# A layernorm–MLP kernel: tile 0's transposes copied in quarters by two engines, tile 2's statistics on ScalarE in place of tile 1's, another product order in the last group, and another packing seed

## Chip, cores, metric

One core of one Trainium2 chip. The metric is the device time of one execution in microseconds, lower is better. A "span" is what the profile of one execution covers; it is about 1.7 us less than the time of that execution. In the lines of a profile PE is TensorE (PEld its weight loads), DVE is VectorE, ACT is ScalarE, POOL is GpSimd; SBUF is the memory for tiles, PSUM the one that TensorE's products are written to.

## The reference

```python
def _layernorm(x, axis=-1, eps=1e-5):
    m = jnp.mean(x, axis=axis, keepdims=True)
    v = jnp.var(x, axis=axis, keepdims=True)
    return (x - m) / jnp.sqrt(v + eps)

def reference(x, w1, b1, w2, b2):        # x (1, 2048, 1024) bf16, w1 (1024, 3584), w2 (3584, 1024)
    y = _layernorm(x, axis=-1)
    h = gelu_tanh(jnp.einsum("bsd,df->bsf", y, w1) + b1)
    return jnp.einsum("bsf,fd->bsd", h, w2) + b2
```

## The kernel before

Both matrix products are done with one level of a seven-product scheme (seven block products P1 to P7 in place of eight, with sums of blocks by VectorE), so VectorE is nearly as busy as TensorE. x comes in 16 tiles of 128 rows. A tile is normalized on VectorE (statistics in two halves, aggregate, plus epsilon; the power -1/2 on GpSimd; then one `tensor_scalar`), or its two moments are taken by ScalarE. The first four tiles are then transposed by TensorE and copied out of PSUM; this is the head.

The program is a list of tasks. A list scheduler fixes each engine's order at build time, from durations and due times written into the kernel, and a packing step with a seed chooses where the buffers lie in SBUF. A buffer that lies on an earlier one's place has to wait for that one's readers.

```python
ACT_LN = (1, 8, 10, 12, 14)       # tiles whose moments ScalarE takes
SEED = 11                          # of the packing
...
def to_yT_pe(b, i, bank, other=None):            # transposes of tile i by TensorE
    ...                                          # tile 0: two halves in banks 7 and 6; others: one bank
    for h in range(2):
        op("ACT", A_CP, lambda e, h=h: e.copy(out=yy[:, h * KH:(h + 1) * KH, t * P:(t + 1) * P],
                                             in_=pv[h][:, h * KH:(h + 1) * KH, :]), ...)
...
elif q == 7:                                     # Wino.step: one product, and what hangs on it
    self.prod(7, Y, False)
    s3 = save(Y, n + "s3", mem=MA)               # ScalarE, PSUM to SBUF
    add(Z, Z, s3, n + "V")                       # VectorE
    if self.last:
        self.s3 = s3
    else:
        MA.free(s3)
    self.sink["22"](Z)                           # output sum and store
elif q == 4 and self.last:                       # last group: P4 as two half tiles
    self.sink["21"](Y, (self.prod, self.s3, (X, (X + 4) % 8)))
...
pr.due = (None, 5.0)                             # the head
norm(0)
pr.due = None
for i in range(1, 4):
    norm(i)
for bank in range(7):
    warm(1, bank=bank, full=True)                # matmuls on ones, to warm TensorE up
warm(20)
for n, c in ((8, c_st[0][0]), (8, c_mv[0]), (6, c_rstd[0])):
    warm(n, c)
to_yT_pe(0, 0, 7, 6)
warm(5, bank=5)
...
flat += [(last, 7), (last, 3), (last, 4)]        # end of the order of products
```

## Time and profile before

| | before |
|---|---|
| time, median of 3 | 335.25 us (335.22 to 335.66) |
| span of the profiled execution | 333.3 us |
| T0, T1, T2 (first weight load of the transposes of tiles 0, 1, 2; the row of their matmuls starts up to 0.06 later) | 6.84, 8.59, 11.32 us |
| M, the first 512-column matmul (the head is over) | 16.49 us |
| E, the end of the last matmul (modelled) | 330.17 us |
| middle, E - M | 313.68 us |
| tail, span - E | 3.1 us |

I cut the time at M and E because the three parts have different causes.

### The profile page before, as it was taken

How to read it: one execution, taken by the hardware profiler on the slowest of the kernel's cores; microseconds unless marked ns; L12 is line 12 of the kernel's file. 1: busy time of each engine (PE TensorE's matmuls, PEld its weight loads, DVE VectorE, ACT ScalarE, POOL GpSimd, SP SyncE). 2: the span in 40 equal slices, each digit the busy share in tenths (PEclk: the TensorE clock that was granted, in tenths of full speed). 3: DMA queues.
4: the chain of work that ended last, by engine and by line, in shares of the span. 5: the costliest groups of instructions: out<-in, count | busy, mean ns of one | idle time of the engine just before them, and what ended most of it. 6: DMA issues, size and time to landing. Idle time of an engine off the chain costs nothing.

```text
span 333.3 us, 6014 instructions
## 1 busy us (share of the span) xinstructions
PE 328.5 (99%) x2328; PEld 220.0 (66%) x2328; DVE 295.9 (89%) x480; ACT 180.9 (54%) x307; POOL 13.0 (4%) x29
## 2 busy tenths in 40 slices
PE   8999999999999999999999999999999999999996
PEld 5844444444444444444446888888888888888885
DVE  5879999999999959968979994999999999999735
ACT  5597999997676776777765555543021222222010
POOL 2210121100000000000000000000000000000000
PEclk9999999999999999999999999999999999999999
DMA  7997999989989998999958462654846547659642
GB/s 228 326 221 183 281 270 328 326 205 305 314 268 365 325 339 260 352 350 325 301 158 245 130 202 76 190 147 141 238 154 187 162 129 208 202 157 269 177 118 63
DMA packets 103622, 76.88 MB, mean 231 GB/s; under 512 B 16426, under 2 KB 94890, under 8 KB 103594
## 3 DMA queue, kind: packets, MB, share of 16 engines
q1 hardware_dynamic: 103034, 76.18, 78.1%
q8 instruction: 18, 0.29, 0.4%
q10 hardware_dynamic: 560, 0.33, 0.3%
q14 instruction: 10, 0.08, 0.1%
HBM read 48.96 MB, written 24.38 MB: 220 GB/s over the span
## 4 chain that ended last, share of the span: by engine, by line
PE 95%; DMA 2%; DVE 1%; SPq 1%; issue 0%; ACT 0%; DVEq 0%
PE ps L891 49%; PE ps L1158 44%; DMA mem<-in_x_dram 2%; PE ps L1220 1%; SPq L754 0%; DVE mem L1078 0%; DVE st_sb L661 0%; PE ps L694 0%; SPq L637 0%; DVE mem L1121 0%; ACT mem L820 0%; DVE mem L670 0%; SPq L634 0%; DVEq L562 0%; PE ps L1180 0%
## 5 line engine op out<-in xcount | busy, mean ns | idle before, releaser
L891 PE MATMUL ps<-mem 128*128 128x512 f16 x756 | 164.3, 379 | 0.0
L1158 PE MATMUL ps<-mem 128*128 128x256 f16 (+1 forms) x1372 | 150.4, 273 | 0.0
L1158 PEld LDWEIGHTS ps<-mem 128*128 128x128 f16 x1372 | 134.2, 98 | 16.4
L891 PEld LDWEIGHTS ps<-mem 128*128 128x128 f16 (+1 forms) x756 | 73.4, 98 | 89.2 <-ACT mem L820 1.4
L820 ACT COPY mem<-ps 128x512 f32<-128x512 f32 x111 | 64.8, 588 | 80.1 <-PE ps L1158 65.5
L804 ACT ACTIVATE mem<-ps,b_sb 128x512 f16<-128x512 f32 x112 | 74.1, 692 | 23.4 <-DVE ps L828 14.2
L828 DVE TENSOR_TENSOR ps<-ps,mem 128x512 f32<-128x512 f32 x84 | 58.3, 693 | 19.3 <-ACT mem L820 19.1
L1048 DVE TENSOR_TENSOR mem<-mem 128x1792 f16<-128x1792 f16 x56 | 59.7, 1083 | 0.9 <-PE ps L1158 0.4
L957 DVE TENSOR_TENSOR mem<-mem 128x512 f16<-128x512 f16 (+5 forms) x84 | 37.0, 461 | 2.7 <-DMA w_scr<-mem 1.4
L765 DVE TENSOR_TENSOR mem<-mem 128x1024 f16<-128x1024 bf16 (+1 forms) x56 | 37.6, 684 | 1.7 <-DMA mem<-in_w_dram 1.6
L1059 DVE TENSOR_TENSOR mem<-mem 128x1792 f16<-128x1792 f16 x32 | 33.9, 1083 | 0.1
L811 ACT COPY ps<-ps 128x512 f32<-128x512 f32 x31 | 17.7, 570 | 27.2 <-PE ps L1158 25.2
L661 DVE BATCH_NORM_STATS2 st_sb<-mem 128x6 f32<-128x512 bf16 x22 | 14.4, 681 | 4.8 <-DMA mem<-in_x_dram 4.8
L1078 DVE TENSOR_TENSOR mem<-ps,mem 128x512 bf16<-128x512 f32 (+1 forms) x25 | 16.2, 663 | 2.7 <-PE ps L1158 2.6
L941 DVE TENSOR_TENSOR mem<-mem 128x2048 f16<-128x2048 bf16 (+1 forms) x16 | 17.3, 1084 | 0.1
L1091 DVE TENSOR_TENSOR mem<-ps,mem 128x512 f32<-128x512 f32 x24 | 16.2, 683 | 0.2
L731 DVE TENSOR_TENSOR mem<-mem 128x512 f16<-128x512 f16 x32 | 12.1, 420 | 1.9 <-DMA mem<-mem 1.7
L667 POOL TENSOR_TENSOR rstd_sb<-vpe_sb,nhalf 128x1 f32<-128x1 f32 x11 | 7.8, 713 | 43.4 <-DVE vpe_sb L664 43.4
L1180 PE MATMUL ps<-ones 128*128 128x128 bf16 (+1 forms) x55 | 6.8, 290 | 1.1 <-POOL ones L603 1.1
L1220 PE MATMUL ps<-mem 128*128 128x128 f16 x112 | 7.3, 219 | 0.2 <-ACT mem L704 0.2
L1220 PEld LDWEIGHTS ps<-mem 128*128 128x128 bf16 x112 | 6.4, 98 | 0.6 <-ACT mem L704 0.5
L856 ACT COPY ps<-mem 128x512 f32<-128x512 f32 x11 | 6.5, 590 | 0.3
(31 smaller groups left out, 59.8 us busy)
## 6 DMA issues: line engine op xcount, KB each, us to landing
mem<-in_w_dram SPq DMA_DIRECT2D x80, 256.0 KB, 4.9
mem<-w_scr SPq DMA_DIRECT2D x28, 448.0 KB, 3.5
w_scr<-mem SPq DMA_DIRECT2D x21, 512.0 KB, 5.0
w_raw<-mem SPq DMA_DIRECT2D x12, 512.0 KB, 5.4
mem<-w_raw SPq DMA_DIRECT2D x12, 448.0 KB, 4.5
mem<-in_w_dram SPq DMA_DIRECT2D x9, 448.0 KB, 4.5
mem<-in_x_dram SPq DMA_DIRECT2D x15, 256.0 KB, 4.4
out_dram<-mem SPq DMA_DIRECT2D x30, 128.0 KB, 2.6
```

The costliest lines, as they stand in the source:

```text
L765: op("DVE", d_tt(n), lambda e: e.tensor_tensor(out=o[0], in0=a[0], in1=bb[0], op=f), r=[a[1], bb[1]], w=[o[1]], name=f"w1S{k}_{ch}")
L804: op("ACT", A_GELU, lambda e: e.activation(out=dst, in_=bank2(bank), func=ACT.Gelu_apprx_tanh, bias=b1_sb[:, f:f + 1], scale=1.0), r=[bank ...
L811: op("ACT", A_CP, lambda e: e.copy(out=banks[dst][:, :], in_=banks[src][:, :]), r=[bank_c[src]], w=[bank_c[dst]], name=name, lat=A_LAT)
L820: op("ACT", A_CP, lambda e: e.copy(out=v16(a, 0, 2048, F32), in_=banks[src][:, :]), r=[bank_c[src]], w=[a.c()], name=name, lat=A_LAT)
L828: op("DVE", D_PS, lambda e: e.tensor_tensor(out=banks[dst][:, :], in0=banks[src][:, :], in1=v16(a, 0, 2048, F32), op=ALU.add), r=[bank_c[s ...
L891: i = e.matmul(banks[bank][:, :], lhsT=lv[:, k, :], rhs=rv[:, k, :], start=(fresh and k == 0), stop=(k == KH - 1), skip_group_check=True)
L941: op("DVE", d_tt(2 * self.n), lambda e: e.tensor_tensor(out=vd, in0=va, in1=vb, op=ALU.subtract), r=self.cells(a) + self.cells(bb), w=self ...
L957: tt = lambda o, a, c: (lambda e: e.tensor_tensor(out=o, in0=a, in1=c, op=ALU.subtract))
L1048: op("DVE", d_tt(UN // 2), lambda e: e.tensor_tensor(out=v16(t), in0=a[0], in1=bb[0], op=f), r=a[1] + bb[1], w=[t.c()], name=f"in{b}_{p}{q}")
L1059: op("DVE", d_tt(UN // 2), lambda e, va=va, vb=vb, vd=vd: e.tensor_tensor(out=vd, in0=va, in1=vb, op=f), r=h_cells(b, a, u, s) + h_cells(b ...
L1158: i = e.matmul(bank2(bank)[:, t, :], lhsT=av3[:, k, t * P:(t + 1) * P], rhs=bv[:, k, :], start=(fresh and t == ts[0] and k == 0), stop=(t ...
L1220: i = e.matmul(banks[r][:, t * P:(t + 1) * P], lhsT=lv[:, k, :], rhs=rhs[:, k, t * P:(t + 1) * P], start=(t == 0 and k == 0), stop=(k == K ...
```

## The change

Its intent, as far as the code tells it: tile 2's normalization no longer stands behind tile 3's load (ScalarE takes tile 2's moments, and the loads go 0, 2, 1, 3); the first transposed tile reaches its matmuls sooner through four quarter copies, two on ScalarE and two on VectorE; and after the last product little is left to do, because P6 and P7, which other sums hang on, come early in the last group and P3, P4 come last.

```diff
-ACT_LN = (1, 8, 10, 12, 14)
+ACT_LN = (2, 8, 10, 12, 14)
-SEED = 11
+SEED = 1
+HEAD_LN = (5.0, 7.3, 9.3, 13.5)
+TE_DUE = 7.1
 ... (eps of a tile on ScalarE: VectorE in place of GpSimd for i < 8)
-            def to_yT_pe(b, i, bank, other=None):
+            def to_yT_pe(b, i, where):
 ...
+                        if j % 2:
+                            op("DVE", 0.11 + m * P / 960, lambda e, src=src, dst=dst: e.tensor_copy(out=dst, in_=src), ...)
+                        else:
+                            op("ACT", 0.15 + m * P / 1400, lambda e, src=src, dst=dst: e.copy(out=dst, in_=src), ...)
 ...
-            pr.due = (None, 5.0)
-            norm(0)
+            for i in range(4):
+                pr.due = (None, HEAD_LN[i])
+                norm(i)
             pr.due = None
-            for i in range(1, 4):
-                norm(i)
 ...
-            to_yT_pe(0, 0, 7, 6)
+            pr.due = (None, TE_DUE)
+            to_yT_pe(0, 0, (7, 6, 5, 4))
 ... (V waits for P5 and P7, whichever is later; s3 kept accordingly)
             flat += [(last, 7), (last, 3), (last, 4)]
+            prev = c_seq[-2]
+            flat[-10:] = [(last, 1), (prev, 7), (last, 6), (prev, 4), (last, 7), (prev, 3), (last, 5), (last, 2), (last, 3), (last, 4)]
 ...
-                    put(i - (IN_LA if q != 3 else 4), lambda b=b, p=p, q=q: in_sum(b, p, q))
+                    at_ = min(i, flat.index((g, 6)) - 1) if q == 5 else i
+                    put(at_ - (IN_LA if q != 3 else 4), lambda b=b, p=p, q=q: in_sum(b, p, q))
```

## The prediction

> **What bounds the kernel now.** I read the page's busy shares first, then the chain that ended last in order of time, then the timeline of the first 17 us, then that of the last 10 us. The busy shares say that the tensor engine is nearly always at work; the chain says where that is not so.
>
> ```profile
> PE 328.5 (99%) x2328; PEld 220.0 (66%) x2328; DVE 295.9 (89%) x480; ACT 180.9 (54%) x307; POOL 13.0 (4%) x29
> ```
> ```profile
> 3.77 5.68 DMA mem<-in_x_dram
> 9.45 0.02 issue
> 9.47 1.28 DVE st_sb L661 x2
> 10.76 0.45 DVE mem L670
> ...
> 16.65 12.95 PE ps L891 x60
> ...
> 63.51 114.29 PE ps L891 x528
> ...
> 186.51 140.62 PE ps L1158 x1288
> 327.13 0.02 issue
> 327.15 0.59 ACT mem L820
> ```
>
> The columns are start, length, engine and line. From 16.65 to 327.13 the chain never leaves PE: 528 matmuls of 512 columns in 114.29 us are 216 ns each, 1288 of 256 columns in 140.62 us are 109 ns each, with no gap. The change alters neither their number nor their shape, so nothing is to be won in those 310 us; it can only be lost. What can move is the head (16.65 us) and what follows the last matmul. In the head the chain runs through the load of x tile 3 (landed at 9.45) and its two statistics on DVE, because the normalization of tile 2 stands behind them in DVE's order: DVE sat 0.94 us waiting for that load, and PE was ready for tile 2's transposes about 0.4 us before it got them.
>
> The timeline of the head (start, length, engine, line, operation; DVE, POOL and PE rows picked):
>
> ```profile
> 5.48 0.15 DVE L664 TENSOR_SCALAR vpe_sb<-mv_sb 128x1 f32<-128x1 f32 x1
> 5.55 0.69 DVE L661 BATCH_NORM_STATS2 st_sb<-mem 128x6 f32<-128x512 bf16 x1
> 5.71 0.56 POOL L667 TENSOR_TENSOR rstd_sb<-vpe_sb,nhalf 128x1 f32<-128x1 f32 x1 [4.17 <-DVE vpe_sb L664]
> 6.31 0.74 DVE L670 TENSOR_SCALAR mem<-mem,mv_sb,rstd_sb 128x512 f16<-128x512 bf16 x2
> 6.84 0.49 PEld L694 LDWEIGHTS ps<-ident,mem 128*128 128x128 f16 x8
> ...
> 7.96 0.67 PEld L1220 LDWEIGHTS ps<-mem 128*128 128x128 bf16 x12 [0.35 <-ACT mem L704]
> 8.00 0.54 DVE L656 TENSOR_SCALAR mem<-mem,mv_sb,rstd_sb 128x1024 f16<-128x1024 bf16 x1
> 8.59 0.49 PEld L694 LDWEIGHTS ps<-ident,mem 128*128 128x128 f16 x8
> ...
> 11.32 0.46 PEld L694 LDWEIGHTS ps<-ident,mem 128*128 128x128 f16 x8 [0.51 <-issue]
> ```
>
> The reader is to see three starts on PE: T0 (tile 0's transposes) 6.84, T1 8.59, T2 11.32. After T2 PE hardly waits, so **the start of T2 is the head's measure**. The timeline of the tail:
>
> ```profile
> 327.77 0.70 DVE L828 TENSOR_TENSOR ps<-ps,mem 128x512 f32<-128x512 f32 x1 [1.45 <-ACT mem L820]
> 328.38 0.68 DVE L1121 TENSOR_TENSOR mem<-mem 128x512 f32<-128x512 f32 x1
> 328.98 1.94 DVE L1078 TENSOR_TENSOR mem<-ps,mem 128x512 bf16<-128x512 f32 x4
> ```
>
> Product P7 ends at 327.13 and what hangs on it (save by ACT, add V, add of s3, four output sums) keeps DVE busy without a gap up to 330.92. PE's last row starts at 304.79 and lasts 25.38, so PE ends at 330.17. The last half-tile sum takes 0.41 us (rows by form), so it started at 330.51: 0.34 us after PE, because of the queue on DVE.
>
> **What the Trainium skill says.** "SBUF — State Buffer", section "Who interferes with whom": DVE and GpSimd share one pair of ports as an exclusive lock. The trace agrees where it shows it: the pow on POOL beside tile 1's normalization took 0.78 us (8.16), the others 0.55 to 0.56. "VectorE: DVE Perf Modes", section "Why PSUM operands drop a tier": a PSUM operand excludes the two-port mode. So the new DVE copies out of PSUM should not hold up POOL; no row of before shows a 16-bit PSUM copy on DVE. "Perfetto Trace Analysis", section "Tensor Engine Instruction (MATMUL, LD_WEIGHTS)": the end of a matmul in a profile is an estimate. Here an output sum began at 325.63, 0.03 us after the end that the chain implies for its product (327.13 less one product of 14 matmuls by 109 ns = 1.53), so the estimate serves within some hundredths.
>
> **The change, part by part.** I took the new order of each engine from the build of the changed kernel (an order, not a time).
>
> *Head, first tile.* DVE did: statistics 0, aggregate 0, eps 0, one half statistic of tile 2, norm 0 (two halves), other half, and so on. It will do: statistics 0, aggregate, eps, both half statistics of tile 1, norm 0. ACT takes tile 2 in place of tile 1 at the same place; tile 2 is now loaded second, tile 1 third, tile 3 fourth, ahead of all weights. Statistics start 0.60 us apart (9.47 to 10.68 for two), so from 5.55 the two are through at 6.76; norm 0 could start at 6.31 and now starts at 6.76. **T0 slips by 0.45, to 7.29.** It gains in copying: first group of matmuls came 1.12 us after T0 (6.84 to 7.96), through a copy of 512 columns. Now ACT copies quarter 0 and DVE quarter 1. A 512-column ACT copy takes 0.59, a 28-column one 0.24, so 256 columns take about 0.41 (interpolated). DVE: norm halves at 6.76 and 7.09, aggregate 7.42, eps 7.67, so the copy starts about 7.75; at 0.41 (the 256-column sum out of PSUM) it ends 8.16. First wave matmul about 8.23, against 7.96: later by 0.27, the quarters giving back 0.18 of 0.45.
>
> *Tile 1.* eps start to norm start is 0.83 on this path (5.48 to 6.31), so with eps 1 at 7.67, norm 1 can start at 8.50; the two DVE copies end about then. Norm 1 to T1 was 0.59 (8.00 to 8.59): T1 at 9.09, 0.50 later than before. After T1: 0.45 to the next matmuls, but the matmuls of tile 1 need its ACT copy, 1.33 after T1 (8.59 to 9.92): 10.42. Then 12 + 4 matmuls at 0.056 (28 in 1.56) make 0.89, so PE is ready for T2 at 11.31.
>
> *Tile 2.* Its statistics are done on ACT at about 6.85. eps 2 follows norm 1 (about 9.05), norm 2 about 9.9, ready at 10.5: no longer late. So T2 starts when PE gets there, 11.31, against 11.32. **Head: gain 0.0.** The wait behind tile 3 goes, and what took its place is the wait for tiles 0 and 1.
>
> *Weights.* Tile 3 now goes ahead of the first weights. Summing bytes moved in half-microsecond windows, the seventh 0.26 MB piece (tile 3 before) passes at 8.1 us and landed at 9.45, 1.3 later; the second passes at 3.85 and landed at 4.42. The first weight tile moves from fourth to fifth place: passes at 6.5, lands about 7.5; the second passes 7.3, lands about 8.5, used at about 8.7. Tight, but I count no wait.
>
> *Tail.* PE's work is the same, its order is P3, then both halves of P4 last, with P5 and P2 ahead of them and P6, P7 long done. Counting back from PE's end E in products of 1.53: P5 ends E-4.59, P2 E-3.06, P3 E-1.53. DVE: W and V from E-4.56 to about E-3.3, the P2 sum from E-3.03, the Z sum E-2.4 to E-1.7, the P3 sum E-1.5 to E-0.8, first half of P4 E-0.74 to E-0.33, then idle until the last half at E+0.03. The start moves from E+0.34 to E+0.03. **Tail: gain 0.31.** The first half of P4 reuses the bank that the P2 sum reads; that is free at about E-2.4, before E-1.53, so no wait.
>
> *Sum:* 0.0 - 0.31 + 0.0 for the middle: 335.25 - 0.31 = 334.94, said as 334.95.
>
> **The rivals.** *A: the slip of norm 0 is absorbed and the head gains.* If tile 1 or 2's data or the POOL steps come sooner, T2 can come up to about 0.4 us earlier, as the wait of 0.36 to 0.51 in front of it goes: 334.5 or so. For it: the change was evidently aimed at that wait. Against: the static order puts both statistics ahead of norm 0, and rows above show no slack of 0.45. *B: weights become the wait.* Fifth to eighth place is later by about 0.8 us each; if the second or third weight tile lands at 9 rather than 8.5, the wave stalls 0.2 to 0.5: about 335.3. The bytes above speak for a near miss. *C: the buffers are packed with another seed, and loads and DVE sums in the middle stand in another order.* DVE is busy 48.91 of 50 us from 50 to 100, so a late load could reach PE. Against it: ACT and PE wait nowhere long in before, and the units for the last group still have some 5 us in hand by the order. It would cost 0.2 to 1 us: 335.2 to 336.
>
> **Range and chances.** The head is uncertain by about 0.3 either way, the tail by 0.1, runs differ by 0.1 to 0.4 (335.22 to 335.66), and C adds a little on the slow side. I take 334.5 to 335.4. Two per cent are 6.7 us; the head's idle and the tail together hold less than that, so faster by 2% is almost excluded (0.01), slower by 2% would need a hang-up in the middle (0.01), within 2% is 0.98.
>
> **What would show it.** T0 near 7.3, first wave near 8.2, T1 near 9.1, T2 near 11.3, no DVE wait for tile 3; the chain no longer through tile 3's load but through tile 0's and 1's statistics; at the end the last two half sums apart, the last starting within 0.1 us of PE's end; PE without gaps between. The prediction is wrong if T2 moves by more than 0.3 us, if a wave waits for weights, or if the middle shows a PE gap.

## More of the kernel before

The middle can be read off one view, the timeline of TensorE alone (start, length, engine, line, operation, count, and in brackets idle time with what ended it):

```profile
16.49 13.11 PE L891 MATMUL ps<-mem 128*128 128x512 f16 x60
29.44 0.38 PE L1180 MATMUL ps<-ones 128*128 128x512 bf16 x1
29.65 148.16 PE L891 MATMUL ps<-mem 128*128 128x512 f16 x684
```

A row ends where TensorE waits or the line changes. One row of 684 matmuls without a bracket means that the profile shows no wait of TensorE there.

## The result

| | before | after |
|---|---|---|
| time, median of 6 runs each | 335.37 us (335.00 to 335.66) | 335.02 us (334.73 to 335.33) |
| ratio | | 0.999, 95% interval 0.9977 to 1.0003 |
| span of the profiled execution | 333.3 us | 333.3 us |
| T0, T1, T2 | 6.84, 8.59, 11.32 | 7.80, 9.65, 11.80 |
| M | 16.49 | 16.99 |
| E - M | 313.68 | 313.73 |
| span - E | 3.1 | 2.6 |

A ratio here is the mean time of one kernel's fast runs over the mean of the other's in the same rounds, so it is not quite the ratio of the medians quoted beside it. The predicted 334.95 and its range hold. In the profiled execution, however, the head lost 0.50 us, which was not predicted, and the tail gave 0.55 back (0.19 of it by chance, as shown below), so the two spans are equal. The experiments had to say which of the two is the change and which is luck.

TensorE's row of 684 is unbroken in this profile too, with the same length:

```profile
30.15 148.19 PE L903 MATMUL ps<-mem 128*128 128x512 f16 x684
```

The chain that ended last, after:

```profile
1.74 4.38 DMA mem<-in_x_dram
6.12 0.02 issue
6.15 1.29 DVE st_sb L664 x2
7.43 0.64 DVE mem L673 x2
...
9.67 0.60 PE ps L700 x8
...
17.15 12.95 PE ps L903 x60
...
187.05 143.68 PE ps L1170 x1316
330.73 0.02 issue
330.75 0.42 DVE mem L1090
```

It no longer passes through tile 3's load. It begins with the third x load (now tile 1), its two statistics and norm 0 (7.43), as the prediction expected of the new order; but the load landed at 6.12, and the prediction had put the start of these statistics at 5.55. At the end one half-tile sum of 0.42 stands behind the last matmul. Before, the chain left TensorE already at P7 (327.13, some 3 us ahead of the last matmul), and a save, two adds and four sums that hang on P7 reached past it.

The timeline of the head, after (VectorE, ScalarE, GpSimd and TensorE rows picked):

```profile
6.15 1.29 DVE L664 BATCH_NORM_STATS2 st_sb<-mem 128x6 f32<-128x512 bf16 x2 [0.83 <-DMA mem<-in_x_dram]
...
7.80 0.72 PE L700 MATMUL ps<-ident,mem 128*128 128x128 f16 x8 [0.80 <-DVE mem L673]
...
8.13 0.70 ACT L712 COPY mem<-ps 128x256 f16<-128x256 f16 x2 [1.43 <-PE ps L700]
...
8.29 0.56 DVE L709 COPY mem<-ps 128x256 f16<-128x256 f16 x2
...
8.46 0.55 POOL L670 TENSOR_TENSOR rstd_sb<-vpe_sb,nhalf 128x1 f32<-128x1 f32 x1 [2.50 <-DVE vpe_sb L667]
...
8.64 0.84 PE L1233 MATMUL ps<-mem 128*128 128x128 f16 x12
```

VectorE sat idle 0.83 us for the load, and TensorE then 0.80 us for norm 0. The quarters work: the copies lie side by side, and the first group of matmuls (8.64) comes 0.84 after T0, against 1.12 before.

The timeline of the tail, after:

```profile
327.70 1.29 DVE L1090 TENSOR_TENSOR mem<-ps,mem 128x512 bf16<-128x512 f32 x2
329.23 1.19 DVE L1090 TENSOR_TENSOR mem<-ps,mem 128x512 bf16<-128x512 f32 x2 [0.24 <-PE ps L1170]
330.75 0.42 DVE L1090 TENSOR_TENSOR mem<-ps,mem 128x256 bf16<-128x256 f32 x1 [0.34 <-PE ps L1170]
```

VectorE idles 0.34 us before the last half sum: it waits for TensorE, and no longer TensorE's result for it. TensorE's last row ends at 330.72, so the sum starts 0.03 after it and ends 0.45 after it. Before, the last half sum ended 0.74 after TensorE's end.

### The profile page after: what moved, and what is told of

It is laid out like the page before. It is cut to its first block, busy times and chain, and to the rows that moved or that the text cites. A ratio compares the mean times of both kernels' runs of the same rounds, so it can differ in the third digit from the quotient of the medians.

```text
span 333.3 us, 6020 instructions
## 1 busy us (share of the span) xinstructions
PE 328.6 (99%) x2328; PEld 220.0 (66%) x2328; DVE 296.6 (89%) x483; ACT 180.3 (54%) x307; POOL 13.8 (4%) x28
## 4 chain that ended last, share of the span: by engine, by line
PE 96%; DMA 1%; DVE 1%; SPq 0%; POOL 0%; issue 0%
PE ps L903 49%; PE ps L1170 45%; PE ps L1233 2%; DMA mem<-in_x_dram 1%; PE ps L700 0%; DVE st_sb L664 0%; DVE mem L673 0%; POOL rstd_sb L670 0%; SPq L639 0%; DVE mem L1090 0%; SPq L636 0%; PE ps L1192 0%; DVE vpe_sb L667 0%; DVE mv_sb L666 0%; PE ps L1245 0%
## 5 line engine op out<-in xcount | busy, mean ns | idle before, releaser
L1170 PEld LDWEIGHTS ps<-mem 128*128 128x128 f16 x1372 | 134.2, 98 | 16.4
L841 DVE TENSOR_TENSOR ps<-ps,mem 128x512 f32<-128x512 f32 x84 | 58.2, 693 | 16.4 <-ACT mem L833 13.0
L1154 ACT COPY ps<-b2d_sb 128x512 f32<-128x512 f32 x6 | 3.5, 590 | 6.0 <-DVE mem L1103 5.8
```

What stands on the lines that cost most here:

```text
L841: op("DVE", D_PS, lambda e: e.tensor_tensor(out=banks[dst][:, :], in0=banks[src][:, :], in1=v16(a, 0, 2048, F32), op=ALU.add), r=[bank_c[s ...
L1170: i = e.matmul(bank2(bank)[:, t, :], lhsT=av3[:, k, t * P:(t + 1) * P], rhs=bv[:, k, :], start=(fresh and t == ts[0] and k == 0), stop=(t ...
```

## The experiments

**Theories.** *Tail only*: the change is worth the shorter queue behind the last product, 0.3 to 0.4 us, and the head is neutral on average. *Late load by order*: the new load order makes the third x load, and with it the head, late in every run; then the head costs 0.5 and half of the tail's gain is lost. *Packing*: the gain comes from seed 1, a better packing. Twelve runs were made, ten of new kernels and two of the changed one; each table row below is cut at M and E as above.

| run | what it is | median us | ratio to before, 95% | M | E - M | span - E |
|---|---|---|---|---|---|---|
| after_again | changed kernel | 334.84 | 0.9987 [0.9966, 1.0007] | 16.43 | 313.8 | 2.6 |
| after_third | changed kernel | 335.17 | 0.9997 [0.9974, 1.0019] | 17.55 | 314.3 | 2.6 |
| tail_only | before + new tail, seed 11 | 343.2 | 1.0231 [1.0208, 1.0253] | 16.83 | 321.9 | 2.6 |
| tail_seed1 | before + new tail, seed 1 | 335.51 | 1.0004 [0.9986, 1.0022] | 16.43 | 314.4 | 2.6 |
| before_seed1 | before, seed 1 | 336.21 | 1.0025 [1.0007, 1.0044] | 16.82 | 314.3 | 2.9 |
| head_only | changed kernel, old tail | 336.07 | 1.0012 [0.9994, 1.0031] | 17.04 | 314.3 | 2.9 |
| norm0_first | changed, tile 1's statistics after norm 0 | 336.47 | 1.0028 [1.0004, 1.0052] | 17.32 | 315.0 | 2.5 |
| act_halves | changed, tile 0 in halves by ScalarE | 335.82 | 1.0007 [0.9987, 1.0026] | 16.60 | 314.9 | 2.6 |
| tile1_act_norm_first | new tail, old tile choice, norms first | 338.91 | 1.0111 [1.0073, 1.0148] | 16.86 | 318.0 | 3.1 |
| tile1_act_interleaved | the same, statistics interleaved, seed 3 | 336.1 | 1.0012 [0.9996, 1.0028] | 16.17 | 316.4 | 2.5 |
| interleaved_seed5 | the same, seed 5 | 335.9 | 1.003 [0.9999, 1.0062] | 16.23 | 315.3 | 2.6 |
| interleaved_seed10 | the same, seed 10 | 336.29 | 1.003 [1.0003, 1.0057] | 16.05 | 316.4 | 2.6 |

M, E - M and span - E are of one profiled execution each. Kernels are compared only within the same rounds.

### after_again: the changed kernel, unaltered

No edit.

> The changed kernel once more, for a second profile of its head. Theory (the new order of loads makes tile 1 land late: three x tiles now follow tile 0 ahead of the weights): tile 1's statistics again start at 6.0 to 6.3 us after a DVE wait of 0.7 us or more, T1 near 9.6, first 512-column matmul near 17.0. Rival (the late landing in the first profile was chance): tile 1 lands by 5.6, T1 near 9.1, first 512-column matmul near 16.5. Time against before: theory 0.999 (some 0.3 us less); rival 0.998 or below.

Here the third load did not hold VectorE (its statistics began at 5.41), and yet T0 came at 7.59. The chain says why:

```profile
1.07 6.73 PE ps L1192 x49
7.80 0.45 PE ps L700 x8
```

Line 1192 is the warm-up. The 49 warm-up matmuls themselves lasted until T0. The view of that line (duration in ns: least, median, greatest) shows that most of their weight loads ran at the slow rate in this execution, and most at the fast one in the profiled execution of the same kernel before it. First this run, then the earlier one:

```profile
L1192 PEld LDWEIGHTS ps<-ones x49: 98/151/152, 1.1 to 7.5; 128*128 128x128 bf16 x49
```
```profile
L1192 PEld LDWEIGHTS ps<-ones x49: 97/98/151, 1.1 to 6.7; 128*128 128x128 bf16 x49
```

From T1 on this execution ran to the prediction: T1 9.09, T2 11.24, M 16.43 (predicted 9.09, 11.31, about 16.5). So the theory that the load is late in every run falls: it is late in some. Nor does the new order of loads show as the reason. By the traces the third x load landed at 5.07 to 6.48 us in the five profiles with the old order (mean 5.65) and at 5.03 to 6.69 in the nine that load tiles 0 to 3 ahead of the weights (mean 5.77).

### tail_only: the last group's order alone, on before

```diff
+            prev = c_seq[-2]
+            flat[-10:] = [(last, 1), (prev, 7), (last, 6), (prev, 4), (last, 7), (prev, 3), (last, 5), (last, 2), (last, 3), (last, 4)]
```
with the changed `Wino.step` and the earlier input sum, and nothing else.

> Only the new order of the last two groups, the head as before. Theory (the whole gain is at the end, and the head takes part of it back): first 512-column matmul near 16.5 as before, PE end to span end 2.6 us in place of 3.1, time 0.5 us below before (ratio 0.9985). Rival (the prediction's sum: 0.3 at the end, nothing in the head): 0.3 us below before (0.9991).

A clear miss: 343.2 us. The tail is as expected (the last half sum again starts 0.03 after TensorE's end), the loss lies almost 180 us before it:

```profile
83.64 70.97 PE L890 MATMUL ps<-mem 128*128 128x512 f16 x328 [0.31 <-DVE mem L765]
159.84 26.55 PE L890 MATMUL ps<-mem 128*128 128x512 f16 x112 [5.24 <-DMA mem<-in_w_dram]
```

TensorE waits 5.24 us for a weight load in a place that the edit does not name. After it some ten matmuls start 0.427 us apart in place of 0.216, as the 512-column ones do in this kernel's warm-up; that costs another 2.2 us. What differs there is the packing. The next run tests that.

### tail_seed1: the same with the other seed

```diff
-SEED = 11
+SEED = 1
```

> Only the new order of the last two groups, head as before, but the buffers packed with the changed kernel's seed. Theory (the end gives 0.5 us, and the 8 us lost with the old seed were packing alone): no PE gap over 0.3 us between the first and the last long matmul (their distance within 0.2 us of 313.5), PE end to span end 2.5 to 2.6, time 0.4 to 0.6 us below before (ratio 0.9985). Rival (the new order at the end forces late loads whatever the packing): PE gaps of some us again, ratio above 1.01.

From tail_only to this kernel only the seed changes, and 7.7 us go. That is shown: the packing's seed decides the middle, by far more than the change is worth. The tail is again the short one, but the middle still has a wait of its own, so the ratio is 1.0004:

```profile
73.67 104.65 PE L890 MATMUL ps<-mem 128*128 128x512 f16 x484 [0.55 <-ACT mem L804]
```

### before_seed1: the seed alone, on before

```diff
-SEED = 11
+SEED = 1
```

> The kernel before with nothing but the seed of the packing changed to 1. Theory (the seed is no gain of its own, it only keeps the packing from costing): time equal to before or up to 1.5 us above it, by PE gaps between 17 and 180 us. Rival (the seed is what made the changed kernel faster): 0.3 us or more below before.

Slower, and the interval excludes 1. The theory that seed 1 is the gain falls: on the old order it costs 0.25%. A TensorE wait that before's profile does not have stands in the middle:

```profile
83.58 95.14 PE L891 MATMUL ps<-mem 128*128 128x512 f16 x440 [0.50 <-DVE mem L765]
```

That this wait comes from the seed is not shown: tail_only, with seed 11, waits for the same line at the same place (83.64), and after_third, the changed kernel unaltered, at 84.36 where its two other profiles do not.

Its T0 also came at 7.69 though norm 0 was done at 6.66: the warm-up was slow here as in after_again, so a late T0 from this cause is no property of the new head.

### head_only: the changed kernel with the old tail

```diff
-            prev = c_seq[-2]
-            flat[-10:] = [(last, 1), (prev, 7), ...]
```
with the old `Wino.step` and input sum.

> Only the head's part of the change (quarters, tile 2 on ScalarE, new due times, new seed), the end as before. Theory: first 512-column matmul near 17.0, PE end to span end 3.1, time 0.3 to 0.5 us above before (ratio 1.001 to 1.0015). Rival (head neutral, as predicted): ratio 1.000.

The tail went back to 2.9 (the last half sum ends 0.74 after TensorE's end, as in before), which fits the theory of the tail. The head was again late: VectorE waited 0.83 us for the third load. The middle is 0.6 longer than in the first profile of the changed kernel. Since after_third shows the same 0.6 with nothing edited, this run does not say that the 0.6 comes from the packing.

### norm0_first: tile 1's statistics held behind norm 0

```diff
                        r=[b.c(h)], w=[c_st[i][h]], name=f"stats{i}_{h}", lat=0.1,
+                       extra=gone[0] if i == 1 else ())
```

> The changed kernel with one order altered on DVE: tile 0's normalization ahead of tile 1's two statistics (they wait for it). Theory (tile 1's own chain, load then two statistics then POOL, sets T1): T0 near 6.6, more than 1 us earlier than in the changed kernel, but T1 still near 9.6 and the time equal to the changed kernel's within 0.1 us. Rival (the late T0 is what costs): T1 and the first 512-column matmul 0.4 us or more earlier, time 0.4 us below the changed kernel's.

T0 came at 7.27, 0.3 to 1.1 earlier than in the runs of the changed kernel; not at the expected 6.6, because the slow warm-up lasted until then. But T1 came at 9.98 and M at 17.32, while in after_again, where the third load had landed equally early (5.09, here 5.03), they came at 9.09 and 16.43. Tile 1's chain (statistics, aggregate, power, norm) sets T1, and to gain on tile 0 by delaying it is a loss. So the order that the change chose, both statistics ahead of norm 0, is right for its choice of tiles.

### act_halves: ScalarE alone copies tile 0, in halves

```diff
-                        if j % 2:
+                        if j % 2 and len(where) > 2:
...
-            to_yT_pe(0, 0, (7, 6, 5, 4))
+            to_yT_pe(0, 0, (7, 6))
```
and tile 3's statistics held behind norm 1.

> The changed kernel, but tile 0's transposes copied by ScalarE in two halves as before (tile 1's normalization kept ahead of tile 3's statistics). Theory (tile 1's chain sets the head, so the quarters are off the path): from the start of tile 0's transposes to the first wave matmul 1.1 us in place of 0.8 to 0.85, but from T1 to the first 512-column matmul still 7.35 and T1 still 3.5 to 3.7 after tile 1's statistics begin; time within 0.1 us of the changed kernel's. Rival (the quarters give 0.25 us): first 512-column matmul later by 0.25 against the start of tile 1's statistics.

From T0 to the first group of matmuls it took 1.11 us, against 0.82 to 0.84 with quarters on two engines: the quarters are worth 0.28 there. But T1 came 3.73 after tile 1's statistics began, against 3.68 in after_again, where the load was early too, and M was 16.60, inside the spread of the changed kernel. Why so little is left: T1 needs norm 1 and the matmuls ahead of it. Here the matmuls came last (norm 1 ended at 8.93, T1 is 9.22); but VectorE, free of the two copies, had ended norm 1 already 3.44 after the start of the statistics, against 3.63 in after_again. One profile each; a gain of 0.1 or 0.2 at M is not excluded.

### tile1_act_norm_first: the old choice of tiles, each norm ahead of the next tile's statistics

```diff
+            AFTER = {(2, 0): 0, (2, 1): 1, (3, 0): 2, (3, 1): 2, (4, 0): 2, (4, 1): 2}
...
+                       extra=gone[AFTER[i, h]] if (i, h) in AFTER else ())
```
on before with the new tail and seed 1.

> A version meant to beat both: the new order at the end, tile 1's statistics on ScalarE as before, and on DVE tiles 0, 1 and 2 normalized ahead of the statistics of the next tiles, so that no normalization stands behind a load. Theory: T0 near 6.9, T1 8.4 to 8.9, T2 10.8 to 11.1, first 512-column matmul 16.0 to 16.3 in place of 16.5 to 17.0, PE end to span end 2.55, time 0.9 us below before (ratio 0.9973). Rival (the head is bound by PE's own work from the first wave on): first 512-column matmul not before 16.5, gain only the 0.5 us of the end.

T0 6.95, T1 8.69, T2 10.88 as wanted, and then the time came due:

```profile
13.72 0.62 PE L700 MATMUL ps<-ident,mem 128*128 128x128 f16 x8 [0.61 <-DVE mem L675]
```
```profile
32.40 150.12 PE L896 MATMUL ps<-mem 128*128 128x512 f16 x684 [2.21 <-DVE mem L737]
```

Tile 3 was late by 0.61, and at 30 us TensorE waited 2.21 us for VectorE's sums over tiles 4 to 7, whose statistics had been pushed back. After that wait, too, the next eight matmuls start 0.42 to 0.43 us apart, which costs another 1.7 us. An early tile bought with later ones was paid back here with interest.

### tile1_act_interleaved, interleaved_seed5, interleaved_seed10: a version meant to beat both

The new tail; tile 1 on ScalarE again; tile 0 in halves by ScalarE; the statistics of tiles 2, 3, 4 set between the norms one half at a time, as an order on VectorE without a wait (and, not in the cut, tile 1's eps back on GpSimd and the first two issues of loads fixed in their order).

```diff
-ACT_LN = (2, 8, 10, 12, 14)
+ACT_LN = (1, 8, 10, 12, 14)
-SEED = 1
+SEED = 3
-HEAD_LN = (5.0, 7.3, 9.3, 13.5)
+AFTER = {'stats2_0': ('norm0',), 'stats2_1': ('norm1',), 'stats3_0': ('eps2',), 'stats3_1': ('norm2',), 'stats4_0': ('eps3',), 'stats4_1': ('norm3',)}
+HEAD_LN = (5.0, 9.5, 10.5, 13.5)
```
The other two differ from it by the seed alone (5 and 10).

> A version meant to beat both: the new tail; tile 1's statistics on ScalarE as before the change; tile 0 copied by ScalarE in two halves; the statistics of tiles 2, 3 and 4 set between the normalizations one half at a time, so that no normalization stands behind a load and no tile's statistics come much later than before; x tiles 0 to 3 loaded in number order ahead of the weights. If the head is set by the order on DVE, T0 comes near 6.9, the first wave near 8.0, T1 near 8.7, T2 near 10.9, T3 with no wait, the main part near 16.1 (before: 16.49, changed kernel 16.43 to 17.0), and the last half-sum 0.03 after PE's end; with the middle unharmed (313.7 from main start to PE's end) the time is 334.3 to 334.6, ratio to before 0.997 to 0.9985. If the rate step of the warm matmuls or the landing of loads binds instead, T0 lies at 7.4 to 7.8 and the main part starts at 16.4 to 16.8: ratio 0.998 to 0.9995. If its packing (another seed, chosen by the kernel's own plan) lengthens the middle by 0.6 to 1.3 as in four earlier runs, the ratio is 1.000 to 1.003.

> The interleaved head again, only the packing seed changed from 3 to 5. The head is the same order, so the main part should start near 16.15 as in the run with seed 3 (T0 6.67, T1 8.84, T3 13.04 there), or up to 16.8 if the warm matmuls' rate step or a load comes late; the last half-sum ends 0.44 to 0.46 after PE's end. The two kernels of this call differ in packing alone, so what differs between them lies between main start and PE's end: 313.7 if nothing stalls, 316.4 with seed 3. If seed 5 leaves the middle unharmed the ratio to before is 0.997 to 0.999; with a loss of 0.6 to 1.3 it is 0.999 to 1.002; with one like seed 3's, 1.004 or more by the profile, though that kernel's median came out at 1.0012.

> The same with packing seed 10. Theory that the packing decides the middle: head within the spread of the seeds 3 and 5 (main start 16.1 to 16.8), tail 0.44 to 0.46, and from main start to PE's end a figure of its own between 313.7 and 316.4, with the stalls on PE between 30 and 90 us at other places than with seed 3 or 5. The rival, that the interleaved order itself makes the later tiles' sums late, expects the same stall in all three seeds: a PE wait on DVE's tile sums near 30 us of about 0.5, and from it the same 0.5 or more lost in the middle.

The head does what was meant: M 16.17, 16.23 and 16.05, the three earliest of all fourteen profiles, with T0 at 6.56 to 6.92. None of the three beat before. In all of them TensorE waits for VectorE's tile sums at the start of the next group; seed 3, 5, 10 in turn:

```profile
29.96 1.25 PE L906 MATMUL ps<-mem 128*128 128x512 f16 x5 [0.47 <-DVE mem L781]
```
```profile
30.47 0.82 PE L906 MATMUL ps<-mem 128*128 128x512 f16 x3 [0.91 <-DVE mem L781]
```
```profile
29.99 1.25 PE L906 MATMUL ps<-mem 128*128 128x512 f16 x5 [0.61 <-DVE mem L781]
```

In before this row began at 29.65, 13.16 after M. Here it begins 13.79, 14.24 and 13.94 after M, so 0.63, 1.08 and 0.78 are lost, more than the 0.26 to 0.44 won at M. The same stall in three packings is what the rival (the order itself makes the later sums late) expected. The rest of the loss in the middle, 0.6 to 2.1 us, has its stalls between 57 and 88 us: some at nearly the same place with two seeds (63.9 and 63.7, 85.1 and 84.3), the others at places of their own. So packing and order both have a share in it that these runs do not separate. No version beats the changed kernel.

### after_third: the changed kernel a third time

No edit.

> The changed kernel once more, unaltered, on the same chip and with five rounds: the gain of the tail alone (0.3 to 0.4 us of 335) gives a ratio of 0.9985 to 0.9995; the head is neutral if the main part starts anywhere between 16.4 and 17.0; T1 to main start 7.3 to 7.4 as in the other new heads; the last half-sum ends 0.44 to 0.46 after PE's end. If the gain were only the luck of single runs, the ratio would lie at 1.000 or above.

The ratio, 0.9997, came out at the near end of what the change can be worth, with an interval wider than the effect. M at 17.55 missed the expected 16.4 to 17.0, by the latest third load of all:

```profile
6.71 1.29 DVE L664 BATCH_NORM_STATS2 st_sb<-mem 128x6 f32<-128x512 bf16 x2 [1.58 <-DMA mem<-in_x_dram]
```

The profiled execution took 336.18 us, the fastest of the same six 334.57. E - M was 314.3 here and 313.7 and 313.8 in the other two profiles of this kernel: some 0.6 of the middle also varies from run to run. This time TensorE's row of 684 is broken by a wait for VectorE:

```profile
84.36 95.14 PE L903 MATMUL ps<-mem 128*128 128x512 f16 x440 [0.21 <-DVE mem L778]
```

## Why the prediction was right, and where it was not

**The bound: right.** Nothing was won in the middle: 313.68 before, 313.73 and 313.8 after, and 314.3 in the third profile.

**The tail, 0.31: right.** From TensorE's end to the end of the last half sum it took 0.74 to 0.75 us in the three profiles with the old order (before, before_seed1, head_only) and 0.45 to 0.46 in all eleven with the new one: 0.29 gained. The last store, of 64 KB, then took 1.67 to 1.68 us from issue to landing with the old order and 1.57 to 1.61 with the new, another 0.08. That it lands sooner because it is less crowded is argued, not shown. From that landing to the end of the span it is 0.42 to 0.52 us in twelve of the fourteen profiles, whatever the order, but 0.67 in before and 1.05 in tile1_act_norm_first. So of the 0.55 between the profiles of before and after 0.37 comes again and 0.19 is chance.

**The head's first step, T0 at 7.29: wrong.** T0 came at 7.80, 7.59 and 8.37. The term that was mis-sized is the start of the statistics of the third load, taken as 5.55 from one execution. By the traces that load landed anywhere from 5.0 to 6.7 us, with either order of loads, so the row behind it cannot start at a fixed time. In one of the three runs of the changed kernel the warm-up matmuls, which the prediction did not have in its sum at all, set T0 instead; over all fourteen profiles they did so, clearly, in five (after_again, tail_seed1, before_seed1, norm0_first, act_halves), 0.4 to 1.35 us after the half of norm 0 that the first transposes need was done.

**The head's later steps: right, counted from the landing.** Predicted M minus the start of those statistics was 16.5 - 5.55 = 10.95. It was 16.99 - 6.15 = 10.84, 17.55 - 6.71 = 10.84, and in head_only 17.04 - 6.21 = 10.83. In after_again, where the load was not late, T1, T2 and M were met within 0.1. The 0.27 by which the first group of matmuls was to slip had one mis-sized term: a 128x256 copy took 0.29 us on VectorE and 0.37 on ScalarE, not 0.41, so the step from T0 to the first group was 0.82 to 0.84, not 0.94.

**"Head: gain 0.0": not contradicted, but the head is more exposed.** With the old order, in tail_only, the third load came at 6.50 and T0 1.06 later. With the new one T0 comes 1.65 after it (7.80 - 6.15, 7.86 - 6.21, 8.37 - 6.71), because both its half statistics, not one, stand ahead of norm 0. A late load thus goes whole into M: 16.43 to 17.55 with the new head (mean of four profiles 17.00), 16.43 to 16.83 with the old (mean of four 16.64). Four each, with such a spread, do not settle whether the mean differs. If it does, it takes back part of the tail's gain.

**By its own signs: partly wrong.** The prediction called itself wrong if T2 moved by more than 0.3 us or if the middle showed a TensorE gap. T2 moved by 0.48 in the profile after, by -0.08 in after_again and by 1.04 in after_third, and after_third has the gap of 0.21 at 84.36. The head's uncertainty, put at 0.3 either way, was too small: M ranged over 1.1 us in three profiles of one kernel.

**Rival A (the head gains): did not come about**, though the interleaved runs show that M can lie 0.3 to 0.4 earlier; it is then lost at 30 us. **Rival B (weights): did not come about**, no row of the changed kernel's head waits for a weight. **Rival C (packing): did not strike this kernel**, but tail_only and before_seed1 show that it strikes near ones, with 8 us and 0.25%. That seed 1 belongs to this plan is luck or search, and the prediction gave it a chance, no more.

**The sum.** The three ratios of the changed kernel are 0.999, 0.9987 and 0.9997, that is 0.34, 0.44 and 0.10 us gained. The prediction's 0.31 lies among them. No single interval excludes 1, so the size of the gain on the clock is not settled; the tail's 0.29 in the traces is. That the median came within 0.07 us of 334.95 is luck: the head and the middle of this kernel vary from run to run by more than that, and in the profiled execution the head's loss and the tail's gain happened to cancel.

**Two statements of the Trainium skill in the prediction** held. The `pow` on GpSimd took 0.55 us beside the VectorE copies out of PSUM (8.46 in the head after), and 0.78 beside a normalization in SBUF in before: these copies did not hold it up. A third statement was there to be used. "VectorE: DVE Perf Modes", section "The TRN2 errata", gives copies from PSUM to SBUF as 120 cycles plus the elements over the mode's factor for VectorE, and 172 plus the elements for ScalarE. At 256 elements that is an estimate of 258 ns (factor 2, 0.96 GHz) and 357 ns (1.2 GHz). Measured in the profile after: 282 to 292 ns and 372 ns. Close, and better than the prediction's interpolation of 0.41 for both.

## What to carry to other kernels

In a kernel with a static order, ask of each step not only how long it takes but whether its start can vary from run to run: an instruction placed ahead of the critical one passes on the whole lateness of the load it waits for. Where buffers are packed by a seed, a part of a change cannot be tried alone by its time; cut the trace into stretches with one cause each and compare those. The work after the last matmul was the one place where this kernel won in every run: 0.3 us from the order of products.

## What the Trainium skill lacked or had wrong

- "TensorE: Matmul & The Clock Gate", section "Part 1: The HAM clock gate", puts the step from the cold to the warm rate at about 4 us of sustained activity, give or take 0.5 us from run to run. Here matmuls ran without pause from 1.07 us, and the spacing of single warm-up matmuls stepped from 107 to 56 ns at about 4.0 us in one profile (tail_only) and at about 6.9 in another (before_seed1), the twelve others between, so 2.9 to 5.8 us after the start. The section does say that the count of slow matmuls varies from run to run; the half microsecond is what is too narrow. The spread was worth about 1 us of T0 (before_seed1: norm 0 done at 6.66, T0 at 7.69). The granted clock that the profile prints did not show it (0.99 to 1.00 throughout).
- "DMA: Bandwidth & Descriptors", section "Anatomy of one DMA — SWDGE (gpsimd) path", fits a fixed cost of about 2.0 us, for transfers that GpSimd issues. It has no such fit for the hardware queues that this kernel uses, where the last stores of 64 KB took 1.6 us from issue to landing, all told; and no figure for how much one and the same load varies from execution to execution: the third 256 KB x load, issued at 1.72 to 1.74 us, landed anywhere between 5.0 and 6.7 us over these fourteen profiles, and in the profile after that decided the head.
